# Retention attention and two MLPs in one kernel: where a chunk's small products, mask, state and key fade stand in a step

## The chip, the cores and the metric

The kernel runs on one core of one Trainium2 chip. The time is device microseconds (us) of one launch, the median of several runs. The engines are named as the profile names them: PE (TensorE, matrix products), PEld (its weight loads), DVE (VectorE), ACT (ScalarE), POOL (GpSimd) and SP (SyncE, which issues the DMAs). Each engine works through its own list of instructions in the order in which the program holds them.

## What is computed

The input is 2 batches of 8 heads with 768 positions of 64 features. Attention runs over blocks of 64 positions with a state per head that decays, and its output goes through two MLPs, one after the other (512 to 2048 to 512, 1536 tokens):

```python
for b in range(nb):                       # 12 blocks of 64 in a sequence
    intra = einsum('bhic,bhjc->bhij', qb, kb) * Dmask
    intra = einsum('bhij,bhjd->bhid', intra, vb)
    inter = einsum('bhid,bhde->bhie', qb * lam_pow, kv_state)
    out[:, :, sl] = intra + inter
    kb_dec = kb * rev_pow                 # the keys fade
    kv_state = lam_block * kv_state + einsum('bhsd,bhse->bhde', kb_dec, vb)

h = x @ w_in;  y = where(h > 0, h, exp(min(h, 0)) - 1) @ w_out      # first MLP
h = y @ w_in;  out = (P(h) / (Q(h) + 1e-6)) @ w_out                 # second MLP
```

## The kernel before, in words

The 1536 tokens are three tiles of 512. The hidden width of an MLP is 16 slices of 128, and one **step** is one slice `f` of one tile `t` of one layer: twelve 128x512 products make the slice `h` (`mlp_h`, line 424), ACT and DVE turn it into `ghi` and `glo` (two halves of the number, for precision), and two steps later twelve products add it to the four accumulators `y` (`mlp_y`, line 506). All products are taken three times, high by high, high by low and low by high.

The attention of the first token tile is done before any step. The attention of the other 1024 tokens, 16 chunks of 64 positions numbered 8 to 23, is laid into the first MLP's steps of `t = 0` and `t = 1`: a **visit** in a step starts chunk `n` and finishes the chunk `d` that the visit before had started. The steps with a visit are written out by hand: 3, 5, 7, 9, 10, 12, 13, 14, 15 for `t = 0` and 2, 4, 6, 8, 10, 12, 14, 15 for `t = 1`. A visit consists of

- `sm_products`: on PE, 64x64 products: keys by queries of `n` (line 332), values by masked scores of `d` (337), faded keys by values of `d` (343), state by queries of `d` (348). They go to two accumulator tiles, `aa`.
- `sm_mask(n)`: on DVE, the scores times the mask (line 368); `sm_decay_q(n)`: on POOL.
- `sm_out(d)`: on ACT, the state is scaled (four instructions, line 378) and the output is copied to `xr` (380); on DVE the new part is added to the state (384), which needs the scaled state and the products of line 343.
- `sm_decay_k(n)`: on ACT, the keys of `n` fade in place (four instructions, line 357). The products of line 343 in the next visit read them.

In the steps of `t = 0` the weights of the first MLP are made as well. They come as 64 bit numbers and are narrowed on DVE (lines 71, 74, 77), then copied on ACT (120) and subtracted on DVE (121). With the activation's own work (ACT lines 437, 438, 441; DVE 439, 442) that is the most work that DVE has in any stage. From step 10 a step makes two half pieces of weights.

The order of all engines in these steps is the order in which the code is written (`manual_schedule`). `run(ops, n)` issues the next `n` operations of a list: `old` holds what is left of the last step's activation (`b` on DVE, `ghi` on ACT, `glo` on DVE), `new` that of this step (`relu`, `exp` on ACT first), `lows` what is left of the last step's weights, and `now` this step's weights. In the kernel before, a step issues `h`; `b` and `ghi` of the step before; the fade of the keys that the last visit began; the first operation of the step's weights and what is left of the last ones; `glo`; `relu` and `exp`; then the visit; then the rest of the weights; and at its end `y` of two steps ago.

The DMAs stand in SP's list in the order of the code as well; the change moves none of them.

Of the kernel before, what the change touches and what calls it, by code (L numbers as in the profile page):

```python
# [29 lines left out]
def fused_kernel(ctx, tc, lam, qkv, w1, w2, ab, out):  # L30
# [5 lines left out]
    NF = w1.shape[0]  # L36
# [254 lines left out]
    chunk = {}  # L291
# [27 lines left out]
    def sm_products(n, d):  # L319

        if not aa_tiles:
            aa_tiles.extend(pa.tile([P, T], F32, tag=f"pa{i}", name=f"aa{i}")
                            .rearrange("p (x m i) -> p x m i", x=2, m=NP) for i in range(2))
            for r in ROWS:
                nc.tensor.matmul(aa_tiles[1][r, 1], lhsT=pick[r], rhs=mask64[r, :, 1:CS + 1],
                                 start=True, stop=True, skip_group_check=True)
            nc.scalar.activation(out=qpow[:, :, 0:CS], in_=aa_tiles[1][:, 1], func=AF.Copy)
        pn, pd = chunk.get(n), chunk.get(d)
        for m in range(NP):
            if pn:  # L330
                for r in ROWS:
                    nc.tensor.matmul(aa_tiles[0][r, 0, m], lhsT=pn["k"][r, m],  # L332
                                     rhs=pn["q"][r, m], start=True, stop=True,
                                     skip_group_check=True)
            if pd:
                for i, r in enumerate(ROWS):
                    nc.tensor.matmul(aa_tiles[1][ROWS[1 - i], 0, m], lhsT=pd["kv"][r, m, 1],
                                     rhs=pd["s"][r, m], start=m == 0, stop=d % KB == 0,
                                     skip_group_check=True)
        for m in range(NP):  # L340
            if pd and d % KB < KB - 1:
                for r in ROWS:
                    nc.tensor.matmul(aa_tiles[0][r, 1, m], lhsT=pd["kv"][r, m, 0],  # L343
                                     rhs=pd["kv"][r, m, 1], start=True, stop=True,
                                     skip_group_check=True)
            if pd and d % KB:
                for i, r in enumerate(ROWS):
                    nc.tensor.matmul(aa_tiles[1][ROWS[1 - i], 0, m], lhsT=state[r, m, 0],
                                     rhs=pd["q"][r, m], start=False, stop=True,
                                     skip_group_check=True)  # L350

    def sm_decay_k(n):

        kv = chunk[n]["kv"]
        if n % KB < KB - 1:
            for m in range(NP):
                nc.scalar.activation(out=kv[:, m, 0], in_=kv[:, m, 0], func=AF.Copy,
                                     scale=mask64[:, m, CS - 1:CS])

    def sm_decay_q(n):  # L360
        q = chunk[n]["q"]
        if n % KB:
            nc.gpsimd.tensor_tensor(out=q, in0=q, in1=qpow[:, :, 0:CS], op=ALU.mult)

    def sm_mask(n):
        b = chunk[n]
        b["s"] = s = ap_.tile([P, NP, CS], F32, tag="s", name=f"s{n}")
        nc.vector.tensor_tensor(out=s, in0=aa_tiles[0][:, 0], in1=mask64[:, :, 0:CS], op=ALU.mult)

    def sm_out(d):  # L370

        t, js = d * CS // T, slice(d * CS % T, d * CS % T + CS)
        if t not in xraw:
            xraw[t] = xr.tile([P, NP, T], F32, tag="xr", name=f"xr{t}")
        first, last = d % KB == 0, d % KB == KB - 1
        if not (first or last):
            for m in range(NP):
                nc.scalar.activation(out=state[:, m, 0], in_=state[:, m, 0], func=AF.Copy,  # L378
                                     scale=qpow[:, m, CS - 1:CS])
        nc.scalar.activation(out=xraw[t][:, :, js], in_=aa_tiles[1][:, 0], func=AF.Copy)  # L380
        if first:
            nc.scalar.activation(out=state[:, :, 0], in_=aa_tiles[0][:, 1], func=AF.Copy)
        elif not last:
            nc.vector.tensor_tensor(out=state[:, :, 0], in0=aa_tiles[0][:, 1],
                                    in1=state[:, :, 0], op=ALU.add)
# [17 lines left out]
    def x_split(layer, t, m):  # L403
        with tc.high_priority(HP):
            if m % 2 == 0:
                x_tiles(layer, t, m // 2)
            hi, lo = xs[layer, t, m]
            src = xraw[t][:, m] if layer == 0 else xraw.pop((t, m))
            split(hi, lo, src, nc.vector)
# [107 lines left out]
    with ExitStack() as actx:  # L517
# [61 lines left out]
        with tc.manual_schedule():  # L579
# [28 lines left out]
            def run(ops, n):  # L608
                for _ in range(n):
                    if ops:  # L610
                        ops.pop(0)()
# [75 lines left out]
        def steps(layer, t):  # L687
            return [(layer, t, f) for f in range(NF)]
# [3 lines left out]
        def att_visit(due, more):  # L692

            n = todo.pop(0) if more and todo else None
            d = due.pop() if due else None
            sm_products(n, d)
            if n is not None:
                sm_mask(n)
                sm_decay_q(n)
                due.append(n)  # L700
            if d is not None:
                sm_out(d)
                del chunk[d]

        with tc.manual_schedule():
            due = []
            faded = []
            lows = w
            old = []
            parks = [(f, i) for f in range(NF) if f not in DIRECT for i in range(2)]  # L710

            park_at = {(1, f): 2 if f in (5, 7, 9, 11) else 1 for f in (0, *range(3, NF - 2))}

            visits = [(3, 5, 7, 9, 10, 12, 13, 14, 15), (2, 4, 6, 8, 10, 12, 14, 15)]
            assert sum(park_at.values()) == len(parks)
            for layer, t, f in steps(0, 0) + steps(0, 1):
                if f == 0 and t:
                    mlp_y(*queue.pop(0))
                    for m in range(NP):
                        x_split(0, t, m)  # L720
                new = mlp_h(layer, t, f, later=True)
                queue.append((layer, t, f))
                if t or f != 1:
                    run(old, 2)
                    for n in faded:
                        sm_decay_k(n)
                    faded = []
                    now = []
                    if t == 0 and 0 < f < FULL:
                        now = [make_pair_ops(f)]  # L730
                        run(now[0], 1)
                    run(lows, 2 if t or f else 0)
                    for _ in range(park_at.get((t, f), 0)):
                        park_w2(*parks.pop(0))
                    if t == 0 and f >= FULL:
                        now = [make_half_ops(*h) for h in ((f + AHEAD, 0), (f, 1)) if h[0] < NF]
                        run(now[0], 1)
                    run(old, 1)
                    run(new, 2)
                    if f == 0 and t == 0:  # L740
                        run(lows, 1)
                        now = [lows]
                else:
                    now = [make_pair_ops(f)]
                    run(old, 1)
                    run(now[0], 1)
                    run(lows, 1)
                    run(old, 1)
                    run(lows, 2)
                    run(old, 1)  # L750
                    run(new, 2)
                    att_hand(*atts[-1])
                if f in visits[t]:
                    att_visit(due, t == 0 or f < NF - 1)
                    faded = list(due)
                for w in now if t or f else ():
                    run(w, len(w) - 1)
                if t == 0 and f + 2 < FULL:
                    load_pair(f + 2)
                elif t == 0 and f >= FULL:  # L760
                    load_raw(2 if f + 2 < NF else 1)
                if loads and (f in visits[t][1 - t:] or t == 0 and f < 2):
                    for load, k in loads.pop(0):
                        load(k)
                lows = [op for w in now for op in w]
                if len(queue) > LAG:
                    mlp_y(*queue.pop(0))
                old = new
            mlp_y(*queue.pop(0))
            for m in range(NP):  # L770
                x_split(0, 2, m)
            run(old, 3)
# [97 lines left out]
```

## Time and profile before

| | |
|---|---|
| median of 3 runs | 580.77 us (580.2 to 581.96) |
| profiled execution | 580.3 us, its span 578.5 us |
| busy over the span | PE 568.9 us (98%), DVE 468.6 us (81%), ACT 358.6 us (62%), POOL 25.2 us (4%) |
| steps of `t = 0` | from about 23 to 126 us of the span |
| steps of `t = 1` | from about 126 to 220 us |

The profile records one execution. A row of a timeline has the start and length of a group of instructions in us, the line of the code, what is written and read, the shape and the count; in square brackets stands how long the engine was idle before it and what it waited for.

### The profile page before, as it was taken

How to read it: one execution, taken by the hardware profiler on the slowest of the kernel's cores; microseconds unless marked ns; L12 is line 12 of the kernel's file. 1: busy time of each engine (PE TensorE's matmuls, PEld its weight loads, DVE VectorE, ACT ScalarE, POOL GpSimd, SP SyncE). 2: the span in 40 equal slices, each digit the busy share in tenths (PEclk: the TensorE clock that was granted, in tenths of full speed). 3: DMA queues.
4: the chain of work that ended last, by engine and by line, in shares of the span. 5: the costliest groups of instructions: out<-in, count | busy, mean ns of one | idle time of the engine just before them, and what ended most of it. 6: DMA issues, size and time to landing. Idle time of an engine off the chain costs nothing.

```text
span 578.5 us, 9311 instructions
## 1 busy us (share of the span) xinstructions
PE 568.9 (98%) x3570; PEld 468.0 (81%) x3570; DVE 468.6 (81%) x742; ACT 358.6 (62%) x687; POOL 25.2 (4%) x43
## 2 busy tenths in 40 slices
PE   8999999799999999999999999999999999999997
PEld 7878887688888888888888888888888888888885
DVE  6999999875667736677988899988898888898882
ACT  3555655666545535555568887676886676776662
POOL 5301000100001000000000000000000000000000
PEclk9999999899999999999999999999999999999999
DMA  8994546665677702553532410000310000200001
GB/s 304 317 271 166 189 122 201 185 178 164 181 251 229 213 25 74 195 187 128 180 110 92 164 36 2 0 1 1 114 32 2 0 1 0 75 1 1 0 1 73
DMA packets 41215, 64.58 MB, mean 112 GB/s; under 512 B 20178, under 2 KB 20178, under 8 KB 41170
## 3 DMA queue, kind: packets, MB, share of 16 engines
q1 hardware_dynamic: 41170, 63.98, 34.6%
q8 instruction: 28, 0.46, 0.3%
q14 instruction: 17, 0.14, 0.1%
HBM read 53.48 MB, written 10.49 MB: 111 GB/s over the span
## 4 chain that ended last, share of the span: by engine, by line
PE 83%; DVE 10%; DMA 2%; ACT 2%; issue 1%; SPq 1%; DVEq 0%; ACTq 0%
PE h L424 39%; PE y L506 37%; PE y L415 3%; DVE w L74 2%; DMA raw<-w_in 2%; DVE w L77 2%; DVE w L121 1%; DVE w L71 1%; ACT w L120 1%; PE aa L332 1%; DVE glo L442 1%; PE aa L343 1%; ACT state L378 1%; DVE b L439 0%; PE pa L195 0%
## 5 line engine op out<-in xcount | busy, mean ns | idle before, releaser
L424 PE MATMUL h<-xhi,w 128*128 128x512 f32 x768 | 205.1, 390 | 0.4 <-DVE w L121 0.4
L506 PE MATMUL y<-ghi,w 128*128 128x512 f32 x712 | 192.7, 393 | 0.0
L424 PEld LDWEIGHTS h<-xhi,w 128*128 128x128 f32 x768 | 143.8, 188 | 31.2 <-DVE w L121 0.9
L506 PEld LDWEIGHTS y<-ghi,w 128*128 128x128 f32 x712 | 132.8, 188 | 27.9
L424 PE MATMUL h<-xlo,w 128*128 128x512 f32 x384 | 102.7, 389 | 0.0
L506 PE MATMUL y<-glo,w 128*128 128x512 f32 x356 | 95.9, 391 | 0.0
L424 PEld LDWEIGHTS h<-xlo,w 128*128 128x128 f32 x384 | 72.1, 188 | 15.0
L506 PEld LDWEIGHTS y<-glo,w 128*128 128x128 f32 x356 | 67.4, 189 | 14.4
L450 ACT ACTIVATE a<-h,babs 128x512 f32<-128x512 f32 x48 | 33.0, 687 | 61.7 <-PE h L424 61.7
L437 ACT ACTIVATE a<-h 128x512 f32<-128x512 f32 x48 | 28.3, 589 | 43.8 <-PE h L424 43.7
L454 DVE SCALAR_TENSOR_TENSOR b<-b,babs,a 128x512 f32<-128x512 f32 x48 | 36.0, 750 | 19.9 <-ACT b L451 19.8
L439 DVE SCALAR_TENSOR_TENSOR b<-a,h 128x512 f32<-128x512 f32 x48 | 32.7, 681 | 13.8 <-ACT a L438 10.7
L441 ACT ACTIVATE ghi<-b 128x512 fp32r<-128x512 f32 x48 | 30.0, 627 | 22.2 <-DVE b L439 22.2
L120 ACT ACTIVATE w<-w 128x512 fp32r<-128x512 f32 (+1 forms) x23 | 18.4, 799 | 38.4 <-DVE w L77 38.4
L442 DVE TENSOR_TENSOR glo<-b,ghi 128x512 fp32r<-128x512 f32 x48 | 33.9, 709 | 7.0 <-ACT ghi L441 5.5
L452 ACT ACTIVATE p<-h,cab 128x512 f32<-128x512 f32 x48 | 37.7, 785 | 0.0
L456 ACT ACTIVATE a<-b,one 128x512 f32<-128x512 f32 x48 | 35.0, 729 | 3.4 <-DVE b L454 2.9
L458 DVE SCALAR_TENSOR_TENSOR p<-p,cab,h 128x512 f32<-128x512 f32 x48 | 35.8, 746 | 1.2
L462 DVE SCALAR_TENSOR_TENSOR b<-b,one,a 128x512 f32<-128x512 f32 x48 | 35.8, 746 | 0.1
L464 DVE SCALAR_TENSOR_TENSOR p<-p,cab,a 128x512 f32<-128x512 f32 x48 | 35.8, 746 | 0.0
L58 DVE TENSOR_TENSOR glo<-p,ghi 128x512 fp32r<-128x512 f32 x48 | 33.0, 688 | 3.0 <-PE y L415 1.5
L457 DVE TENSOR_TENSOR p<-p,h 128x512 f32<-128x512 f32 x48 | 32.8, 682 | 2.9 <-ACT p L452 2.9
(87 smaller groups left out, 631.0 us busy)
## 6 DMA issues: line engine op xcount, KB each, us to landing
raw<-w_in SPq DMA_DIRECT2D x64, 512.0 KB, 4.3
att<-qkv_in SPq DMA_DIRECT2D x16, 256.0 KB, 5.5
qk<-qkv_in SPq DMA_DIRECT2D x16, 256.0 KB, 3.9
kv<-qkv_in SPq DMA_DIRECT2D x64, 64.0 KB, 3.5
w2d<-wp SPq DMA_DIRECT2D x16, 256.0 KB, 4.3
w<-w2d SPq DMA_DIRECT2D x16, 256.0 KB, 2.7
x2d<-o SPq DMA_DIRECT2D x12, 256.0 KB, 2.2
x2r<-x2d SPq DMA_DIRECT2D x12, 256.0 KB, 3.3
```

Of the source, the lines that this page charges most:

```text
L58: lo_eng.tensor_tensor(out=lo, in0=src, in1=hi.bitcast(F32), op=ALU.subtract)
L424: nc.tensor.matmul(h, lhsT=w[:, a, 0, k * P:(k + 1) * P], rhs=xs[layer, t, k][b], start=i == k == 0, stop=i == 2 and k == NP - 1)
L442: lambda: nc.vector.tensor_tensor(out=glo, in0=b, in1=ghi.bitcast(F32), op=ALU.subtract)]
L450: nc.scalar.activation(out=a, in_=h, func=AF.Abs, scale=babs[:, 0:1])
L452: nc.scalar.activation(out=p, in_=h, func=AF.Identity, scale=cab[:, 3:4], bias=cab[:, 2:3])
L454: nc.vector.scalar_tensor_tensor(out=b, in0=b, scalar=babs[:, 1:2], in1=a, op0=ALU.mult, op1=ALU.add)
L456: nc.scalar.activation(out=a, in_=b, func=AF.Ln, bias=one[:, 0:1])
L457: nc.vector.tensor_tensor(out=p, in0=p, in1=h, op=ALU.mult)
L458: nc.vector.scalar_tensor_tensor(out=p, in0=p, scalar=cab[:, 1:2], in1=h, op0=ALU.add, op1=ALU.mult)
L462: nc.vector.scalar_tensor_tensor(out=b, in0=b, scalar=one[:, 0:1], in1=a, op0=ALU.add, op1=ALU.mult)
L464: nc.vector.scalar_tensor_tensor(out=p, in0=p, scalar=cab[:, 0:1], in1=a, op0=ALU.add, op1=ALU.mult)
L506: nc.tensor.matmul(ys[layer, t][m], lhsT=w[:, a, 1, m * P:(m + 1) * P], rhs=g[b], start=f == i == 0, stop=False)
```

## The change

Three things move, and no instruction is added or taken away. The visit's products stand ahead of the step's `h` on PE. The mask, the fade of the queries, the state and the copy to `xr` come as a list, `rest`, and are issued right after `b` and `ghi` of the step before, ahead of the step's weights and of `relu`. The fade of the keys, which stood in the step after the visit behind `ghi`, is issued at the end of the visit's own step, behind its weights (for the last visit of `t = 0`, at the end of the first step of `t = 1`).

```diff
             d = due.pop() if due else None
             sm_products(n, d)
+            rest = []
             if n is not None:
-                sm_mask(n)
-                sm_decay_q(n)
+                rest += [lambda: sm_mask(n), lambda: sm_decay_q(n)]
                 due.append(n)
             if d is not None:
-                sm_out(d)
-                del chunk[d]
+                rest += [lambda: sm_out(d), lambda: chunk.pop(d)]
+            return rest
...
+                rest = att_visit(due, t == 0 or f < NF - 1) if f in visits[t] else []
                 new = mlp_h(layer, t, f, later=True)
                 queue.append((layer, t, f))
                 if t or f != 1:
                     run(old, 2)
-                    for n in faded:
-                        sm_decay_k(n)
-                    faded = []
+                    while rest:
+                        rest.pop(0)()
                     now = []
...
-                if f in visits[t]:
-                    att_visit(due, t == 0 or f < NF - 1)
-                    faded = list(due)
                 for w in now if t or f else ():
                     run(w, len(w) - 1)
+                if f in visits[t] and f < NF - 1 or f == 0 and t:
+                    for n in due:
+                        sm_decay_k(n)
```

Two places show what that does to the engines' lists. The first is DVE and ACT around step 5 of `t = 0`, which has a visit. `b_0_4`, `ghi_0_4` and `glo_0_4` belong to the activation of step 4, `w_4` and `w_5` are weights, `s` is the masked score, `a_0_5` the activation of step 5 (lines 437 and 438 are `relu` and `exp`). DVE before:

```order
L439 SCALAR_TENSOR_TENSOR b_0_4_674<-a_0_4_673,h_0_4_658 128x512
L71 TENSOR_SCALAR w_5_726<-raw_5_643 128x1024
L121 TENSOR_TENSOR w_4_681<-w_4_682,w_4_681 128x1024
L442 TENSOR_TENSOR glo_0_4_672<-b_0_4_674,ghi_0_4_671 128x512
L368 TENSOR_TENSOR s_764<-aa_624,dmask 128x256
L384 TENSOR_TENSOR state<-aa_624,state 128x4x64
L74 SCALAR_TENSOR_TENSOR w_5_726<-raw_5_643,w_5_726 128x1024
```

DVE now:

```order
L439 SCALAR_TENSOR_TENSOR b_0_4_678<-a_0_4_677,h_0_4_662 128x512
L368 TENSOR_TENSOR s_757<-aa_598,dmask 128x256
L384 TENSOR_TENSOR state<-aa_598,state 128x4x64
L71 TENSOR_SCALAR w_5_768<-raw_5_647 128x1024
L121 TENSOR_TENSOR w_4_681<-w_4_682,w_4_681 128x1024
L442 TENSOR_TENSOR glo_0_4_676<-b_0_4_678,ghi_0_4_675 128x512
L74 SCALAR_TENSOR_TENSOR w_5_768<-raw_5_647,w_5_768 128x1024
```

The mask and the add to the state stand directly behind `b`; three operations that stood ahead of them now stand behind. ACT at the same place, before:

```order
L120 ACTIVATE w_4_681<-w_4_682 128x1024
L441 ACTIVATE ghi_0_4_671<-b_0_4_674 128x512
L437 ACTIVATE a_0_5_721<-h_0_5_706 128x512
L438 ACTIVATE a_0_5_721<-a_0_5_721 128x512
L378 ACTIVATE state<-state,qpow 128x64 x4
L380 ACTIVATE xr_767<-aa_625 128x4x64
```

and now:

```order
L120 ACTIVATE w_4_681<-w_4_682 128x1024
L441 ACTIVATE ghi_0_4_675<-b_0_4_678 128x512
L378 ACTIVATE state<-state,qpow 128x64 x4
L380 ACTIVATE xr_760<-aa_599 128x4x64
L437 ACTIVATE a_0_5_753<-h_0_5_738 128x512
L438 ACTIVATE a_0_5_753<-a_0_5_753 128x512
```

The scaling of the state still stands behind `ghi` of step 4, which reads what `b` wrote. The second place is steps 12 and 13 of `t = 0`, which both have a visit: visit 12 begins chunk 13, and visit 13 reads its keys. ACT before, where `kv_1135` holds the keys of chunk 13:

```order
L120 ACTIVATE w_12_1231<-w_12_1_1233 128x512
L441 ACTIVATE ghi_0_12_1223<-b_0_12_1226 128x512
L357 ACTIVATE kv_1135<-kv_1135,dmask 128x64 x4
L437 ACTIVATE a_0_13_1310<-h_0_13_1295 128x512
L438 ACTIVATE a_0_13_1310<-a_0_13_1310 128x512
L378 ACTIVATE state<-state,qpow 128x64 x4
```

and now, where they are `kv_1139`:

```order
L120 ACTIVATE w_12_1260<-w_12_1_1262 128x512
L357 ACTIVATE kv_1139<-kv_1139,dmask 128x64 x4
L441 ACTIVATE ghi_0_12_1247<-b_0_12_1250 128x512
L378 ACTIVATE state<-state,qpow 128x64 x4
L380 ACTIVATE xr_760<-aa_599 128x4x64
L437 ACTIVATE a_0_13_1346<-h_0_13_1331 128x512
```

The fade has passed one instruction, `ghi`; it still stands behind the copy of the last weights of step 12. PE at the same place, from the end of step 12 on, before:

```order
L506 MATMUL y_0_3_585<-ghi_0_10_1083,w_10_1090 128x512
L424 MATMUL h_0_13_1295<-xhi_0_0_263,w_11_1180 128x512 x2
L424 MATMUL h_0_13_1295<-xhi_0_1_299,w_11_1180 128x512 x2
...
L332 MATMUL aa_624<-qk_1140 64x64 x2
L337 MATMUL aa_625<-s_1262,kv_1135 64x64 x2
...
L343 MATMUL aa_624<-kv_1135 64x64 x2
L348 MATMUL aa_625<-qk_923,state 64x64 x2
```

and now:

```order
L506 MATMUL y_0_3_585<-ghi_0_10_1107,w_10_1117 128x512
L332 MATMUL aa_598<-qk_1144 64x64 x2
L337 MATMUL aa_599<-s_1253,kv_1139 64x64 x2
...
L343 MATMUL aa_598<-kv_1139 64x64 x2
L348 MATMUL aa_599<-qk_927,state 64x64 x2
...
L424 MATMUL h_0_13_1331<-xhi_0_0_263,w_11_1180 128x512 x2
L424 MATMUL h_0_13_1331<-xhi_0_1_299,w_11_1180 128x512 x2
```

The twelve products of `h` that stood between the end of step 12 and the read of the faded keys now stand behind that read.

## Rows read from the trace of the kernel before

**Rows 1.** Waits of PE: engine, line, releaser; us in total, times, longest

```profile
PE aa L343 <- ACT kv L357: 3.4, 1, 3.4
```

**Rows 2.** Windows: length, busy us and instructions by engine, clock, DMA share, GB/s

```profile
27.00:80.00 53.00, 52.55 (x425) 41.84 (x425) 50.25 (x62) 31.58 (x67) 3.28 (x4) 1.00 0.72 212
80.00:99.00 19.00, 19.00 (x170) 15.45 (x169) 17.03 (x27) 10.16 (x20) 0.73 (x1) 1.00 0.51 155
...
105.00:109.00 4.00, 4.00 (x32) 3.16 (x29) 2.78 (x6) 2.60 (x9) 0.00 (x0) 0.57 0.50 140
...
110.00:225.00 115.00, 115.00 (x1059) 93.75 (x1058) 73.41 (x128) 61.72 (x152) 7.34 (x9) 1.00 0.59 177
```

**Rows 3.** Chain of waits from 20 to 110 us, its shares by line

```profile
by line: DMA raw<-w_in 15.3%; DVE w L74 14.9%; DVE w L77 12.8%; DVE w L121 7.8%; issue 6.9%; ACT w L120 5.4%; DVE w L71 5.1%; PE y L506 4.9%; DVE glo L442 4.9%; ACT state L378 3.4%; DVE b L439 3.2%; SPq L315 2.6%; ACT ghi L441 1.7%; ACT a L
```

**Rows 4.** Timeline of PE, end of step 12 to step 14

```profile
94.84 1.19 PE L506 MATMUL y<-ghi,w 128*128 128x512 f32 x4
...
97.70 1.07 PE L424 MATMUL h<-xhi,w 128*128 128x512 f32 x4
...
100.51 0.27 PE L332 MATMUL aa<-qk 64*64 64x64 f32 x2
...
104.60 0.27 PE L343 MATMUL aa<-kv 64*64 64x64 f32 x2 [3.40 <-ACT kv L357]
...
105.72 2.07 PE L506 MATMUL y<-ghi,w 128*128 128x512 f32 x4
...
110.01 1.08 PE L424 MATMUL h<-xhi,w 128*128 128x512 f32 x4
...
113.35 0.23 PE L343 MATMUL aa<-kv 64*64 64x64 f32 x2
```

**Rows 5.** Timeline of DVE, steps 4 to 13

```profile
48.55 0.68 DVE L442 TENSOR_TENSOR glo<-b,ghi 128x512 fp32r<-128x512 f32 x1
...
51.54 0.68 DVE L439 SCALAR_TENSOR_TENSOR b<-a,h 128x512 f32<-128x512 f32 x1
...
54.50 0.42 DVE L368 TENSOR_TENSOR s<-aa,dmask 128x256 f32<-128x256 f32 x1
55.37 0.42 DVE L384 TENSOR_TENSOR state<-aa,state 128x256 f32<-128x256 f32 x1 [0.46 <-ACT state L378]
...
67.30 0.42 DVE L384 TENSOR_TENSOR state<-aa,state 128x256 f32<-128x256 f32 x1 [0.46 <-ACT state L378]
...
79.22 0.42 DVE L384 TENSOR_TENSOR state<-aa,state 128x256 f32<-128x256 f32 x1 [0.28 <-ACT state L378]
...
83.16 1.23 DVE L121 TENSOR_TENSOR w<-w,w 128x1024 fp32r<-128x1024 f32 x1 [0.53 <-ACT w L120]
...
107.40 0.42 DVE L384 TENSOR_TENSOR state<-aa,state 128x256 f32<-128x256 f32 x1 [1.17 <-ACT state L378]
```

**Rows 6.** Timeline of ACT, steps 4 to 14

```profile
47.28 0.61 ACT L441 ACTIVATE ghi<-b 128x512 fp32r<-128x512 f32 x1
47.79 1.05 ACT L357 ACTIVATE kv<-kv,dmask 128x64 f32<-128x64 f32 x4
48.75 0.58 ACT L437 ACTIVATE a<-h 128x512 f32<-128x512 f32 x1
...
52.63 0.61 ACT L441 ACTIVATE ghi<-b 128x512 fp32r<-128x512 f32 x1
53.15 0.58 ACT L437 ACTIVATE a<-h 128x512 f32<-128x512 f32 x1
...
54.29 1.05 ACT L378 ACTIVATE state<-state,qpow 128x64 f32<-128x64 f32 x4
...
103.68 0.63 ACT L441 ACTIVATE ghi<-b 128x512 fp32r<-128x512 f32 x1
104.22 1.05 ACT L357 ACTIVATE kv<-kv,dmask 128x64 f32<-128x64 f32 x4
...
112.11 1.05 ACT L357 ACTIVATE kv<-kv,dmask 128x64 f32<-128x64 f32 x4
```

More of the change, by code (lines that the diff above doesn't have):

```diff
@@ L724, in fused_kernel @@
                     run(old, 2)
-                    for n in faded:
-                        sm_decay_k(n)
-                    faded = []
+                    while rest:
+                        rest.pop(0)()
                     now = []
```

## The prediction, made before the changed kernel was run

> **What bounds the kernel now.** I read the waits of PE first. After the start-up PE stops once for more than half a us, for 3.4 us, before the products of line 343, and what it waits for there is the fade of the keys on ACT, line 357 [rows 1]. From that point on it runs without a break, and the end of the kernel is this run's end. So whatever makes PE late up to that point is paid in full, and nothing else is.
>
> The second view is the windows. DVE works 50.25 of 53.00 us from 27 to 80 us and 17.03 of 19.00 us from 80 to 99 us, but only 73.41 of 115 us from 110 to 225 us [rows 2]. PE looks as full as DVE in the first two, but it is not what sets the pace: the chain of waits from 20 to 110 us is made of DVE's weight lines 74, 77, 121 and 71, of the weights' DMAs and of ACT's lines 120 and 378, with PE's `y` at 4.9% [rows 3]. PE started the stage with work in hand, and DVE falls behind it step by step until at step 13 PE has used up its lead. I read the timelines around that point last.
>
> There, PE finishes `y` (94.84 to 97.70) and `h` (97.70 to 100.51, 2.81 us), issues the first part of visit 13 and waits from about 101.2 until the first of the four fades of chunk 13 is done: 104.60 [rows 4]. On ACT that fade stands behind `ghi` of step 12, which starts at 103.68; the fade itself starts at 104.22 [rows 6]. [...]
>
> **The change, part by part.** The work of PE is the same, and each `h` and `y` has a visit before it as often as before, so the order on PE costs nothing where PE doesn't wait. SP's list keeps its order. In `t = 1` DVE has a third of its time free [rows 2], and its visits are two steps apart but for the last; I take nothing there. What is left is `t = 0`.
>
> *The add to the state.* On DVE it now stands right behind `b` and the mask, ahead of weights that need nothing from it. It needs the scaled state, and the scale on ACT stands behind `ghi`, which in turn needs `b`. In step 5: `b` starts at 51.54 and takes 0.68, the mask 0.42 [rows 5], so DVE is at the add at 52.64. On ACT `ghi` starts at 52.63, and the next instruction at 53.15 [rows 6]; the scale now comes there, takes 1.05 [rows 6], and the add can start at about 54.22. DVE idles 1.58 us. Before, the add stood behind three more operations and idled 0.46 [rows 5]: 1.12 us more. Step 7 has the same spacing and the same 0.46, step 9 the same spacing with 0.28, so 1.30 [rows 5]. Together 3.5 us. The visit of step 10 has no add, since it finishes a sequence; there the mask fills 0.3 us of a wait of 0.53 us [rows 5]. Net 3.2 us. From below, a visit costs nothing more if the scale could be ready when DVE arrives; nothing in the lists allows that, since the scale can't pass `ghi`. From above, the rows' lengths overlap a little at their ends, so that DVE may be there some 0.1 us earlier in each visit.
>
> [...] The row shows that DVE stood still for 0.46 us before the add although weight operations were behind it [rows 5]. [...]
>
> *The fade ahead of `ghi`.* The four fades take 0.96 us until the next instruction (47.79 to 48.75) and now stand ahead of `ghi`. In step 4 `ghi` moves from 47.28 to 48.24 and ends at 48.85 with its 0.61 [rows 6]; `glo` on DVE, which reads it, started at 48.55 [rows 5] and now waits 0.3 us. That happens in steps 4, 6 and 8: 1.0 us. From below it is nothing, if DVE arrives later for another reason.
>
> So DVE, and with it ACT, is 4.2 us later at step 12 than before.
>
> *Visit 13.* The fade gains the place of `ghi`, 104.22 to 103.68, 0.54 us [rows 6]. But the products stand ahead of `h` now. PE arrives at the fade 0.7 us (100.51 to 101.2) after 97.70, at about 98.4 instead of 101.2 [rows 4], and can't do `h` while it waits; `h`, 2.81 us, which before ran ahead of the wait, comes after it. So the end of the step moves by 4.2 - 0.54 + 2.81 = 6.5 us. Bounds of this term by itself: 2.27 us if DVE is not late at all.
>
> *Visits 14 and 15.* Both follow a step with a visit. DVE's mask now waits for PE. In step 13, `b` is done when `ghi` starts, 103.68 [rows 6]; the products end 1.12 us after 104.06 (104.60 to 105.72 [rows 4]), at 105.18; the mask ends at 105.6, the scale 1.05 later than 105.18, and the add starts at about 106.25. DVE idles 1.5 + 0.65 = 2.2 us where it idled 1.17 [rows 5]: another 1.0 us. The fade for visit 14 began at 112.11 [rows 6] and is now at 112.11 + 4.2 - 0.54 + 1.0 = 116.8, its four parts done from 117.1 to 117.9. PE comes to it at 113.35 [rows 4] + 6.5 - 2.81 = 117.0, and the four pairs of products wait for the four parts, 0.4 to 0.5 us in all. Visit 15 repeats this. Together 0.9 us; nothing from below, if the lists leave the 0.6 us that they lack, and 2 us from above, DVE's whole loss in two steps.
>
> [...]
>
> **Sum.** 4.2 + 2.3 + 0.9 = 7.4 us on the profiled 580.3: 587.7. The median of the runs is 0.5 above the profiled execution, so 588.2.
>
> **Rivals.**
> - *DVE's loss is swallowed.* DVE waits for DMAs in this stage too (15.3% of the chain [rows 3]); if these waits shrink by as much as the others grow, only 2.3 remain: 583.1. Against it: a DMA of raw weights goes out when DVE frees its buffer, so it moves with DVE. Chance 0.12.
> - *A second cold stretch.* [...] Chance 0.14. [...]
> - *Faster: the stall goes.* The fade is issued a step earlier in the code. [...] The point that decides is the copy of the last weights of step 12 on ACT: the fade stands right behind it and can't start before 103.68, and PE comes at 98.4. DVE would have to be 5.3 us earlier. Chance 0.06.
> - *No difference.* The change is made of moves on engines with slack but for DVE: 580.8. It needs gains and losses to cancel. Chance 0.04.
>
> **The numbers.** The main case has 0.64, with 585.5 to 590 as its own range. The range of 583.5 to 592 takes in the cold stretch, 2 us for visits 14 and 15, and most of the case in which part of DVE's loss is swallowed; outside it are a little under 0.2. A difference of 0.3%, 1.7 us, is about what a measurement of this kernel can tell from none. Faster 0.06, same 0.04, slower 0.90.
>
> **What would show it.** In the profile after: a wait of PE before line 343 at visit 13 of 5 us or more, now ahead of `h`; waits of DVE before line 384 in steps 5, 7 and 9 of about 1.6 us, released by line 378; short waits of `glo` for `ghi` in steps 4, 6, 8; DVE 4 us later at step 12; 0.3 to 0.5 us waits of PE before line 343 in steps 14 and 15; no new wait from 130 us on. It is wrong if DVE at step 12 is as early as before, or if PE at visit 13 finds the keys faded.

## The result, and the profile after

The changed kernel takes 589.63 us (588.37 to 590.62, 4 runs) against 581.37 us (580.2 to 582.16, 4 runs) of the kernel before on the same chip: a ratio of 1.0139 [1.0118, 1.0159], 1.4% slower. The forecast was 588.2 us. The profiled execution took 588.37 us with a span of 586.6 us, where the one of before took 580.3 and 578.5: 8.1 us more in the span, and these 8.1 us are what has to be found.

The waits of PE, in the view that [rows 1] are taken from (line, releaser, us in total, times, longest):

```profile
PE aa L343 <- ACT kv L357: 5.8, 1, 5.8
PE h L424 <- DVE w L121: 1.5, 2, 0.8
...
PE aa L332 <- DVE state L384: 0.8, 1, 0.8
PE aa L332 <- ACT state L382: 0.5, 1, 0.5
```

The one wait for the faded keys has grown from 3.4 to 5.8 us. The other three lines are small: two are new, and line 424 waited 0.4 us before. All of them lie ahead of that wait, so they take from it and not from the end: a PE that comes earlier to line 343 waits there longer, until the same fade is done.

The windows (length, busy us and instructions of PE, PEld, DVE, ACT, POOL, then clock, DMA share, GB/s), against [rows 2]:

```profile
27.00:80.00 53.00, 51.49 (x416) 40.83 (x415) 47.89 (x58) 28.64 (x60) 5.50 (x4) 1.00 0.66 205
...
105.00:109.00 4.00, 0.31 (x12) 0.31 (x15) 3.23 (x6) 1.86 (x5) 0.00 (x0) 0.50 0.43 154
109.00:115.00 6.00, 6.00 (x44) 4.80 (x37) 4.53 (x9) 2.09 (x8) 0.00 (x0) 0.51 0.40 117
130.00:225.00 95.00, 95.00 (x854) 77.52 (x853) 57.30 (x100) 49.19 (x120) 5.13 (x7) 1.00 0.60 176
```

DVE, which sets the pace from 27 to 80 us, does 2.36 us less work in these 53 us (47.89 against 50.25, 58 instructions against 62). From 105 to 109 us PE works 0.31 of 4.00 us at half the clock (0.50), and from 109 to 115 us it is busy throughout, still at half (0.51). The forecast and the expectations call such a stretch cold; in the kernel before, with 0.57 from 105 to 109 us [rows 2], the `y` that began in it took 4.29 us, 1.43 more than the 2.86 of the `y` of the step before [rows 4]. From 130 us on it is busy 95.00 of 95.00 us: nothing is lost there.

The timeline of DVE shows where its work went; the brackets give the idle time ahead of an instruction and its releaser:

```profile
48.89 0.89 DVE L442 TENSOR_TENSOR glo<-b,ghi 128x512 fp32r<-128x512 f32 x1 [0.25 <-ACT ghi L441]
52.69 0.42 DVE L368 TENSOR_TENSOR s<-aa,dmask 128x256 f32<-128x256 f32 x1
54.77 0.42 DVE L384 TENSOR_TENSOR state<-aa,state 128x256 f32<-128x256 f32 x1 [1.67 <-ACT state L378]
...
68.42 0.42 DVE L384 TENSOR_TENSOR state<-aa,state 128x256 f32<-128x256 f32 x1 [1.67 <-ACT state L378]
...
82.06 0.42 DVE L384 TENSOR_TENSOR state<-aa,state 128x256 f32<-128x256 f32 x1 [1.67 <-ACT state L378]
...
103.09 0.93 DVE L71 TENSOR_SCALAR w<-raw 128x512 int32<-128x512 int32 x1 [0.63 <-DMA raw<-w_in]
```

Steps 5, 7 and 9 lose 1.67 us each before the add, where they lost 0.46, 0.46 and 0.28 [rows 5]; `glo` waits 0.25 us in step 4. The last row is a wait for a DMA, 0.63 us in step 12. All of DVE's waits from 27 to 105 us (us in total, times, longest):

```profile
DVE state L384 <- ACT state L378: 5.0, 3, 1.7
DVE w L71 <- DMA raw<-w_in: 1.5, 3, 0.7
DVE glo L442 <- ACT ghi L441: 0.7, 3, 0.3
DVE w L121 <- ACT w L120: 0.2, 1, 0.2
```

The same view of the kernel before has 1.2 us for the add (three times), 0.5 for line 121, none for `glo`, and for the DMA

```profile
DVE w L71 <- DMA raw<-w_in: 2.5, 3, 1.3
```

so that DVE waits 7.4 us in this stretch where it waited 4.2. Of the 1.0 us by which the waits for the DMA are shorter, 0.55 lie at one wait at about 35 us and are made up again by step 4, whose `b` starts at 46.19 before and at 46.20 now; from there on DVE waits 1.2 us for the DMA before and 0.8 now. The timeline of ACT says why the add waits, and when the keys of chunk 13 are ready:

```profile
53.17 0.61 ACT L441 ACTIVATE ghi<-b 128x512 fp32r<-128x512 f32 x1
53.69 1.05 ACT L378 ACTIVATE state<-state,qpow 128x64 f32<-128x64 f32 x4
...
107.77 0.63 ACT L120 ACTIVATE w<-w 128x512 fp32r<-128x512 f32 x1 [1.16 <-DVE w L77]
108.30 1.05 ACT L357 ACTIVATE kv<-kv,dmask 128x64 f32<-128x64 f32 x4
```

The scale starts 0.52 us after `ghi` and the add 1.08 us after the scale, while DVE was done with the mask at about 53.1. The fade stands right behind the copy of the last weights and begins at 108.30; it was at 104.22 [rows 6]. Last PE, from the end of step 12 on, against [rows 4]:

```profile
102.19 0.27 PE L332 MATMUL aa<-qk 64*64 64x64 f32 x2 [0.54 <-ACT state L382]
...
108.69 0.37 PE L343 MATMUL aa<-kv 64*64 64x64 f32 x2 [5.81 <-ACT kv L357]
...
109.83 2.07 PE L424 MATMUL h<-xhi,w 128*128 128x512 f32 x4
...
115.02 1.09 PE L506 MATMUL y<-ghi,w 128*128 128x512 f32 x4
...
117.87 0.27 PE L332 MATMUL aa<-qk 64*64 64x64 f32 x2
...
134.32 1.07 PE L424 MATMUL h<-xhi,w 128*128 128x512 f32 x4
```

Line 343 starts at 108.69 where it started at 104.60: 4.1 us. Step 13 ends at 117.87, 9.18 us later; before it ended at 110.01, 5.41 us later: 3.8 us. The last row shown is the first `h` of `t = 1`. In the kernel before it was

```profile
126.27 1.07 PE L424 MATMUL h<-xhi,w 128*128 128x512 f32 x4
```

so it is now 8.05 us later, and the steps 14 and 15 added only 0.2 us. 4.1 + 3.8 + 0.2 = 8.1, the whole difference of the spans.

### The profile page after: what moved, and what is told of

Same layout as the page of the kernel before. It is cut to its first block, busy times and chain, and to the rows that moved or that the text cites. A ratio compares the mean times of both kernels' runs of the same rounds, so it can differ in the third digit from the quotient of the medians.

```text
span 586.6 us, 9301 instructions
## 1 busy us (share of the span) xinstructions
PE 572.7 (98%) x3570; PEld 471.3 (80%) x3570; DVE 468.0 (80%) x742; ACT 358.5 (61%) x687; POOL 26.3 (4%) x43
## 4 chain that ended last, share of the span: by engine, by line
PE 82%; DVE 8%; DMA 4%; ACT 2%; issue 1%; SPq 1%; ACTq 0%; DVEq 0%
PE h L424 39%; PE y L506 36%; PE y L415 3%; DMA raw<-w_in 2%; DVE w L74 2%; DVE w L77 2%; DVE w L121 1%; DVE glo L442 1%; DMA att<-qkv_in 1%; DVE w L71 1%; PE aa L332 1%; PE aa L343 1%; ACT w L120 1%; DMA kv<-qkv_in 1%; SPq L178 1%
## 5 line engine op out<-in xcount | busy, mean ns | idle before, releaser
L424 PE MATMUL h<-xhi,w 128*128 128x512 f32 x768 | 208.7, 395 | 1.5 <-DVE w L121 1.5
L506 PE MATMUL y<-ghi,w 128*128 128x512 f32 x712 | 189.7, 389 | 0.0
```

What stands on the lines that cost most here:

```text
L424: nc.tensor.matmul(h, lhsT=w[:, a, 0, k * P:(k + 1) * P], rhs=xs[layer, t, k][b], start=i == k == 0, stop=i == 2 and k == NP - 1)
L506: nc.tensor.matmul(ys[layer, t][m], lhsT=w[:, a, 1, m * P:(m + 1) * P], rhs=g[b], start=f == i == 0, stop=False)
```

## Experiments

They came in three batches, each on a chip of its own and beside its own runs of the kernel before: 581.87 us for e1 to e4, 581.7 for e5 to e8, 581.51 for e9 to e12. The ratios given are to these. The theory was that of the forecast: DVE loses by the add's new place, PE loses because `h` no longer covers the wait for the keys. The rivals were that the fade's place alone does it, that the clock does it, and that DMAs stand behind all of it.

### The parts of the change: e1, e2, e3

e1 does one part alone, on the kernel before:

```diff
-                    for n in faded:
-                        sm_decay_k(n)
-                    faded = []
...
                     att_visit(due, t == 0 or f < NF - 1)
-                    faded = list(due)
                 for w in now if t or f else ():
                     run(w, len(w) - 1)
+                if f in visits[t] and f < NF - 1 or f == 0 and t:
+                    for n in due:
+                        sm_decay_k(n)
```

> Of the three moves only the fade of the keys is made: it is issued at the end of the visit's step, ahead of ghi; products, mask and state stay where they were before. Theory of the prediction: the fade gains the 0.54 us of ghi at visit 13, and glo waits 0.25 us in steps 4, 6 and 8 (0.8 us in all), so 0.2 to 0.5 us slower than before, about 581.7; the wait of PE before line 343 stays at 3.4 to 3.9 us and stands behind h. Rival 1: an earlier fade takes the wait away, 576.5. Rival 2: most of the 8.3 us of the change come from the fade standing ahead of ghi, 586 or more.

Measured 583.13 us, 1.0025 [1.0008, 1.0043]. The wait before line 343 stays at 3.3 us; there is a second of 1.5 us before line 332. The fade's new place by itself brings nothing and costs about 1.3 us, where 0.2 to 0.5 were expected. That is little more than the measurement can tell from none, and in the profiled execution DVE waited 2.5 us for raw weights from 40 to 105 us, where the kernel before waited 1.2.

e2 keeps the products ahead of `h`, but puts mask, state and copy back behind `relu` and `exp`:

```diff
                     run(old, 2)
-                    while rest:
-                        rest.pop(0)()
                     now = []
...
                     att_hand(*atts[-1])
+                while rest:
+                    rest.pop(0)()
                 for w in now if t or f else ():
```

> The changed kernel with mask, queries' fade, state and x back behind relu and exp of the step; the products ahead of h and the fade at the end of the step stay. Theory of the prediction, term by term: DVE's adds wait as little as before, so its 3.2 us go, and 1.0 for glo, 2.3 for h behind the wait, 0.9 for visits 14 and 15 and the longer cold stretch stay: about 586. Rival: the moves hang together. With the products at the head of a step, the mask and the state of the visit before must be through by then, and where visits stand in consecutive steps (9 and 10, 12 to 15) the products wait for DVE: waits of 2 us each before lines 332 and 343 at visits 10, 14 and 15, and a time as long as that of the changed kernel or longer, 589.5 to 592.

Measured 597.84 us, 1.0279 [1.0257, 1.03]: both the theory and the rival missed, by 5.8 us and more. The timeline of ACT in step 13, and of DVE there and in the two steps behind it:

```profile
113.97 0.60 ACT L437 ACTIVATE a<-h 128x512 f32<-128x512 f32 x1 [4.37 <-PE h L424]
...
115.14 1.05 ACT L378 ACTIVATE state<-state,qpow 128x64 f32<-128x64 f32 x4
```

```profile
116.22 0.42 DVE L384 TENSOR_TENSOR state<-aa,state 128x256 f32<-128x256 f32 x1 [5.57 <-ACT state L378]
...
129.44 0.42 DVE L384 TENSOR_TENSOR state<-aa,state 128x256 f32<-128x256 f32 x1 [5.94 <-ACT state L378]
...
139.99 0.42 DVE L384 TENSOR_TENSOR state<-aa,state 128x256 f32<-128x256 f32 x1 [5.61 <-ACT state L378]
```

`relu` needs the step's `h`, `h` now stands behind the visit's products, and these wait for the fade. So the scale behind `relu` comes very late, DVE stands still for 5.6 to 5.9 us in three steps, and PE's waits before line 343 are 8.5 us in three. The change's two moves belong together: with the products ahead, "rest ahead" is worth 8.2 us (597.84 against 589.63), although it is what makes DVE wait 1.67 us in steps 5, 7 and 9.

e3 shortens that wait alone: in the changed kernel the scale goes to the head of the step, ahead of `ghi`.

```diff
+                done = due[:1] if f in visits[t] else []
...
                 if t or f != 1:
+                    for d in done:
+                        sm_scale(d)
                     run(old, 2)
```

> The changed kernel with the four scalings of the state (line 378 there, in its own function here) issued on ACT at the head of the step, ahead of ghi, so that DVE's add finds them done. Theory of the prediction: the waits of DVE before the add in steps 5, 7 and 9 fall from 1.67 us to under 0.5, DVE is 3 to 3.5 us earlier at step 12, and all of that is won at visit 13: 586 to 587. Rival (the DMAs of the weights set DVE's pace, its waits are swallowed): the waits fall, the time stays at 589 to 590.

Measured 587.55 us, 1.0097 [1.0077, 1.0116], 2.1 us below the changed kernel's median. In the timeline of DVE, steps 5 and 12:

```profile
54.45 0.42 DVE L384 TENSOR_TENSOR state<-aa,state 128x256 f32<-128x256 f32 x1 [1.15 <-ACT state L372]
...
103.09 0.47 DVE L71 TENSOR_SCALAR w<-raw 128x512 int32<-128x512 int32 x1 [1.89 <-DMA raw<-w_in]
```

The add still waits 1.15 us, not the expected 0.5 or less, since the scale now stands behind the copy of the last weights (line 120). The waits of the three steps are 3 x 0.52 = 1.6 us shorter, and the median is 2.1 us lower: it lies between the theory (586 to 587) and the rival (589 to 590), so DVE's wait before the add is paid at the end in the main. In the profiled execution most of it was lost again. Line 71 of step 12 starts at 103.09 in both kernels, here after 1.89 us of waiting for the raw weights, there after 0.63. On SP the group of loads that begins with the one for that line starts, in the changed kernel and in e3,

```profile
98.52 9.57 SPq L107 DMA_DIRECT2D raw<-w_in  x4
```

```profile
97.26 10.37 SPq L107 DMA_DIRECT2D raw<-w_in  x4
```

so the load was sent 1.26 us earlier, and line 71 started 5.8 us behind it instead of 4.6. The load went out earlier with DVE, but how long DVE waits there changes from one execution to the next (0.63 to 2.21 us with the same program up to it: e4 and e12, below).

### Where in the run: e7 and e8

The new order in steps up to 12 of `t = 0` only (e7), and from step 13 on only (e8):

```diff
+                ahead = t == 0 and f < 13
+                rest = att_visit(due, t == 0 or f < NF - 1) if f in visits[t] and ahead else []
...
-                if f in visits[t]:
-                    att_visit(due, t == 0 or f < NF - 1)
-                    faded = list(due)
+                if f in visits[t] and not ahead:
+                    for op in att_visit(due, t == 0 or f < NF - 1):
+                        op()
```

The cut is against the kernel before. In e8 the first line reads `ahead = t or f >= 13`; the fade is at the end of the step in both.

> Half of the change: in steps 3 to 12 of t = 0 as in the changed kernel, in visits 13 to 15 of t = 0 and in t = 1 products behind h, and mask, state and x behind relu and exp, as before; the fade at the end of the step everywhere. Theory of the prediction: DVE's 4.2 us less the 0.54 of ghi stay, h runs ahead of the wait again, so its 2.81, the 0.9 of visits 14 and 15 and the longer cold stretch go: before + 3.7, 585.3. Rival (the loss is made at the consecutive visits alone): within 1.5 us of before, 581.5 to 583.

> The other half: steps 3 to 12 of t = 0 with products behind h and the rest behind relu and exp, as before; visits 13 to 15 of t = 0 and all of t = 1 as in the changed kernel; the fade at the end of the step everywhere. Theory of the prediction: h behind the wait 2.81, less 0.54 for ghi, 0.8 for glo, 0.9 for visits 14 and 15, 0.9 for the longer cold stretch: before + 4.9, 586.5. Rival (the loss is DVE's adds in steps 5 to 9, the place of h is nothing): 581.5 to 583.

Measured 585.82 us, 1.0085 [1.0065, 1.0105], and 586.17 us, 1.0084 [1.0066, 1.0101]. Both expectations held. The halves cost 4.1 and 4.5 us, together 8.6 against 8.3 for the whole. The fade's move is in both; counted once, with the 1.3 us of e1, they make 7.3. By the intervals of the three runs, about 1 us each, both sums fit the whole. The waits of PE in e7, the longest line:

```profile
PE aa L343 <- ACT kv L357: 4.2, 1, 4.2
```

and in e8:

```profile
PE aa L332 <- ACT state L382: 4.1, 1, 4.1
PE aa L343 <- ACT kv L357: 3.3, 1, 3.3
```

In e7 `h` still runs ahead of the wait, and PE waits because DVE, and with it the fade, is late. In e8 nothing ahead of step 13 has a new place but the fade, and PE loses by its own order: it stands at the visit's products twice, with `h` behind both waits. The first of these waits comes from the seam between the two orders (in the changed kernel it is 0.5 us), but the second ends with the fade in any case.

### The clock: e4 and e12

Both fill PE's wait at visit 13 of the changed kernel with products of 128x256 whose result nobody uses, 28 in e4 and 44 in e12:

```diff
+        for _ in range(44 if d == 13 else 0):
+            nc.tensor.matmul(aa_tiles[1][:, 1].rearrange("p m i -> p (m i)"), lhsT=wt[0, 11][:, 0, 0, 0:P], rhs=xs[0, 0, 0][0][:, 0:NP * CS],
+                             start=False, stop=True, skip_group_check=True)
```

The lines below them are shifted by three: 343 is 346 here, 357 is 360, 424 is 427.

> The changed kernel with 28 extra 128x256 products on PE at visit 13, between the products of lines 337 and 343, where PE waits 5.8 us; they go to a part of an accumulator that is not read again, so they add work whose result is not used. [...]

> The changed kernel with 44 instead of 28 extra 128x256 products in PE's wait at visit 13, so that some 5.2 of the 5.8 us are filled; their result is not used. With 28 they took 3.6 us, 2.3 us of idle time were left, and a cold stretch of 3.4 us came all the same, later and in the products of h and y. Theory: idle time under 1 us brings no lower clock, h of step 13 takes 2.8 us instead of 5.2, and the time falls by 1.5 to 2.5 us to 587 to 588. Rival: DVE sets the pace through steps 13 to 15 and hides what the clock costs: 589 to 590.5.

e4: 589.76 us, 1.0139 [1.0111, 1.0167]. The products ended while PE still had 2.3 us to wait, and the clock fell all the same, later (0.74 from 109 to 115 us). That says nothing on what the clock costs. e12: 590.75 us, 1.015 [1.0116, 1.0185]. Its windows and the two groups that count on PE's timeline:

```profile
103.00:109.00 6.00, 5.66 (x58) 5.39 (x48) 4.98 (x8) 1.53 (x4) 0.74 (x1) 1.00 0.29 96
109.00:115.00 6.00, 5.98 (x54) 4.97 (x55) 4.19 (x8) 3.67 (x11) 0.00 (x0) 1.00 0.52 136
```

```profile
110.02 1.19 PE L427 MATMUL h<-xhi,w 128*128 128x512 f32 x4
...
112.87 1.07 PE L509 MATMUL y<-ghi,w 128*128 128x512 f32 x4
...
117.83 0.27 PE L346 MATMUL aa<-kv 64*64 64x64 f32 x2 [1.46 <-ACT kv L360]
...
118.82 0.96 PE L427 MATMUL h<-xhi,w 128*128 128x512 f32 x3
```

At the full clock (1.00) `h` of step 13 takes 2.85 us (110.02 to 112.87) and not 5.19. But PE then waits 1.46 us for the fade of the next chunk, and `h` of step 14 starts at 118.82, in the changed kernel at 118.97. In the profiled executions the gain is 0.2 us (588.18 against 588.37), not 1.5 to 2.5: DVE and ACT set the pace through steps 13 to 15, and the PE at half clock mostly spent what it would have waited. Line 71 of step 12 started 0.5 us later in this execution than in that of the changed kernel (103.59 against 103.09), so that much of a gain may be hidden in it. The median, 1.1 us above the changed kernel's and 0.25 above the rival's range, says less than it seems to: in two of e12's four executions (591.73 and 591.96 us) the mean clock was 0.996, so, by that mean, some stretch at a lower clock was in them too. The other two, at 1.000, took 588.18 and 589.78 us, within the 588.37 to 590.62 of the changed kernel, whose clock was 0.991 to 0.994. A gain of 2 us is not there; one below 1 us can't be ruled out.

The changed kernel, e4 and e12 have the same program up to that line, and yet DVE waited there for the raw weights 0.63, 1.62 and 2.21 us. A difference of a us in this one wait is no effect of an edit.

### The fade early, and what stands behind it: e5, e6, e9, e10, e11

Line 343 waits since the fade stands on ACT behind the copy of weights that DVE makes. e5 puts it inside the visit, right behind the state and the copy, in the order of before; e6 does the same to the changed kernel (behind `relu` and `exp`):

```diff
                     att_visit(due, t == 0 or f < NF - 1)
-                    faded = list(due)
+                    for n in due:
+                        sm_decay_k(n)
                 for w in now if t or f else ():
```

> The kernel before with one move: the fade of the keys is issued inside the visit, right behind state and x and so ahead of the step's copies of weights on ACT, which wait for DVE. Theory: at visit 12 ACT has some 2 us of slack there and the keys have landed, so they are faded when PE comes to visit 13; its wait of 3.4 us and the cold stretch of 1.43 us behind it go, DVE's lateness shows in small waits elsewhere: 577 to 578.5 against 581.6 before. Rival: at visits 13 and 14 the keys of the new chunk have only just been sent for, ACT waits for their DMA with the copies of the weights behind it, and the gain goes there: 580.5 to 582.

> The changed kernel with the fade issued right behind relu and exp of the visit's step, ahead of the copies of the weights. Theory of the prediction: PE's wait at visit 13 falls from 5.8 us to about 1 and the cold stretch behind it (2.3 us) goes; DVE's losses at the adds stay and show as waits of PE for keys, masks or weights: 583.5 to 585.5. Rival: DVE's lateness is what PE waits for in any case, so that the wait only moves to other lines: 587 to 589.5.

e5: 581.95 us, 0.9996 [0.9977, 1.0015], the rival's number. e6: 590.42 us, 1.0155 [1.0131, 1.018]: the theory missed by 5 us, the rival by 1. The waits of PE in e5, its longest line, and the two fades on ACT's timeline:

```profile
PE aa L332 <- DMA qk<-qkv_in: 3.2, 2, 2.5
```

```profile
110.04 1.07 ACT L357 ACTIVATE kv<-kv,dmask 128x64 f32<-128x64 f32 x4 [1.09 <-DMA kv<-qkv_in]
...
117.51 1.06 ACT L357 ACTIVATE kv<-kv,dmask 128x64 f32<-128x64 f32 x4 [1.17 <-DMA kv<-qkv_in]
```

The wait before line 343 is gone from e5, the clock is 1.00 from 103 to 115 us, and the time has not moved: PE waits 3.2 us for the DMA of the next chunk's queries and keys, and ACT for that of the keys and values. The same lines of e6:

```profile
PE aa L332 <- DMA qk<-qkv_in: 5.2, 2, 4.6
PE h L424 <- DVE w L121: 2.6, 3, 1.2
PE aa L337 <- DMA kv<-qkv_in: 2.0, 1, 2.0
```

The chunk's loads stand in SP's list behind the loads of raw weights, which wait for a buffer that DVE must free (from 84 to 112 us of the kernel before, SP waits there 14.1 us for line 71). e10 turns the two around on the kernel before, and nothing else; e9 is e5 with that, e11 is e6 with it:

```diff
-                elif t == 0 and f >= FULL:
-                    load_raw(2 if f + 2 < NF else 1)
                 if loads and (f in visits[t][1 - t:] or t == 0 and f < 2):
...
                         load(k)
+                if t == 0 and f >= FULL:
+                    load_raw(2 if f + 2 < NF else 1)
```

> The control to the run above: the kernel before with the order of these loads alone. Theory: PE's wait at visit 13 is for the fade behind the copies of the weights, not for loads; it stays at 3.4 us, 581 to 582.5. Rival: the loads alone give the gain, 577 to 579; or raw weights are late, 583 and more.

> The kernel with the fade inside the visit, products and state in the order of the kernel before, and in steps 10 to 15 the loads of the next chunk's keys, values and queries ahead of the loads of raw weights on SP, which wait there for DVE. Theory: the wait of 3.4 us for the fade at visit 13 only moved to waits for the next chunk's DMAs, on PE 2.5 us for queries at visit 15 and on ACT 1.1 and 1.2 us for keys, because these loads stand behind raw loads that wait for DVE; with them ahead, nothing takes the place of the wait: 576.5 to 578.5. Rival: raw weights come later by the 2.5 to 3.8 us that SP needs for the six loads, DVE waits that much more for them in steps 11 and 12, and the time stays at 581 to 583.

> The changed kernel with both, the fade right behind relu and exp and the loads first. Theory: of the 8.3 us of the change, what hangs on the fade at visit 13 goes (PE's wait of 5.8 us with h behind it, the long cold stretch), and no DMA takes its place as it did with the fade alone; DVE's waits at the adds in steps 5, 7 and 9 stay and show at weights, masks and state, 2.5 to 4 us: 582.5 to 585. Rival: DVE's lateness is in the end of the stage anyway: 588 to 590.

The times of all three lie in the theory's ranges. e10: 581.16 us, 1.0005 [0.9983, 1.0026] (PE's wait before line 343 was 2.2 us at visit 13 in its profile, not 3.4, and 0.8 us at visit 15), so the order of the loads alone is worth nothing. e9: 578.06 us, 0.9928 [0.9904, 0.9952], 3.5 us faster than before and the fastest of all. e11: 584.87 us, 1.0055 [1.0035, 1.0075], 4.8 us below the changed kernel. The waits of PE in e9 and its window from 105 to 109 us:

```profile
PE aa L332 <- DVE state L384: 1.0, 1, 1.0
PE h L424 <- DVE w L121: 1.0, 1, 1.0
```

```profile
105.00:109.00 4.00, 4.00 (x78) 3.16 (x76) 3.63 (x9) 3.48 (x12) 0.39 (x1) 1.00 0.67 193
```

PE is busy 4.00 of 4.00 us, where it worked 0.31 in the changed kernel, and at a clock of 1.00, where the kernel before had 0.57 and the changed kernel 0.50. The waits of PE in e11:

```profile
PE h L424 <- DVE w L121: 3.0, 3, 1.2
PE aa L332 <- DVE state L384: 1.8, 2, 1.2
...
PE aa L343 <- ACT kv L357: 1.1, 2, 0.7
```

With the same two cures the new order is still 6.8 us behind e9, and its longest waits are now for DVE. The cures together take 3.5 us off the kernel before and 4.8 us off the changed kernel; neither gains by the fade alone (e5, e6). So the late fade explains little of the difference between the two orders by itself: of the 8.3 us of the change 6.8 are left when the keys come in time. The forecast's terms that need no late fade, 4.2 us for DVE and 0.9 for visits 14 and 15, make 5.1 of them; the other 1.7 us are not explained by these runs.

## Why the prediction was right or wrong, point by point

- **What bounds the kernel, and that only lateness at visit 13 counts:** right for these two kernels. The span grew by 8.1 us, the first `h` of `t = 1` came 8.05 us later, and PE ran without a break behind it. e9 shows the other side: with that wait gone, and the loads behind it, the kernel is 0.7% faster than before.
- **The add to the state, 3.5 us:** 1.67 us against 0.46, 0.46 and 0.28 make 3.8. The spacing from `ghi` over the scale to the add was read rightly, and step 10's mask fills a wait as forecast (0.53 to 0.20). Two weight operations (lines 71 and 121), which ran without a wait when they stood there before, stood behind the add, and DVE started neither while it stood still for 1.67 us: in step 5 its rows come in the order of its list (`b` 52.09, mask 52.69, add 54.77, line 71 55.11, line 121 55.71).
- **The fade ahead of `ghi`, 1.0 us:** 0.25, 0.24 and 0.24, so 0.7.
- **DVE and ACT 4.2 us later at step 12, the fade 0.54 us earlier in its list:** the sum, 3.66, measured 4.08 (104.22 to 108.30): DVE's `b` of step 12 is 4.68 us later (102.97 to 107.65), and the fade gains 0.60. From `b` of step 4 on, the waits alone make 3.8: 3.8 for the add, 0.7 for `glo`, less 0.3 for line 121 and 0.4 for the DMA. The other 0.9 are lengths of single instructions, on which the forecast had nothing: the three `glo` that wait take 0.89 or 0.90 us instead of 0.68 (0.6 in all), line 71 of step 12 0.93 instead of 0.43, and others are shorter. That the waits and the lengths together come close to the forecast's 4.2 is in part luck. e7, which has this half and the fade's move, cost 4.1 us in the median.
- **`h` behind the wait, 2.81 us:** the step that the sum rests on, and right in kind: from line 343 to the end of step 13 it is 3.77 us more. The excess is the clock (0.50 to 0.51 up to 115 us). `h` took 5.19 us (109.83 to 115.02) instead of 2.81, and the `y` behind it 2.85 (115.02 to 117.87) instead of 4.29: 2.81 + 2.38 - 1.44 = 3.75.
- **Visits 14 and 15, 0.9 us:** 0.2, and PE does not wait there. The forecast 2.81 + 0.9 = 3.7 and the measured 3.77 + 0.2 = 4.0 stand for the same time: the half clock spent what PE would have waited at visit 14. e12 bears it out: at a clock of 1.00 the wait is there, 1.46 us, and `h` of step 14 starts within 0.2 us of the same time.
- **The clock, and a second cold stretch (0.14):** the sum has no term for the clock, which is wrong in the profile and nearly right in the time. The stretch was longer, 9.9 us at half clock from 105 to 115 us against 3.4 before, and `h` took 2.4 us more in it; but by e12's profile that cost 0.2 us at the end, or 0.7 with line 71's 0.5 us. The four executions of the changed kernel point the same way: the two with the lower mean clock, 0.991, took 588.37 and 589.39 us, the two with 0.994 589.87 and 590.62.
- **The swallowed loss (0.12):** 0.4 of the 4.2 us by which DVE's other waits grew, in the profiled execution (1.2 us of waits for the DMA from step 4 on before, 0.8 after); that is less than this wait changes between executions, so it is not shown to come from the change. There was never more than 1.2 to take in that stretch, which the share of 15.3% of the chain [rows 3] hid: it counts the transfers, not DVE's waits.
- **Faster, the stall goes (0.06):** the point named was that the fade stands behind the last weights' copy. It does, and e5 shows that even without it the time stays, because the DMAs of the next chunk come next (PE waits 3.2 us for its queries and keys). That second limit was not seen in the forecast or ahead of e6; only the rival of e5 named it.

So the mechanism was right and the sum 0.7 us short in the span: 0.4 at the fade's start, 0.3 in the steps behind it. What stays open is how the 6.8 us between e11 and e9 divide between the add and the other moves, and why DVE waits 0.63 us for the raw weights of step 12 in one execution and 2.21 in another.

## What to carry to other kernels

Work that an engine can do while something else is late is cover, and a waiting instruction that is moved ahead of it puts all of it on the path: `h` cost nothing ahead of the wait, and behind it its 2.8 us stood in the sum in full. On the engine that sets the pace, an instruction is worth no earlier place than its slowest input allows: the add held DVE up for 1.67 us in each of three steps. And when a wait is taken away and the time does not move, look for the next wait and cure both: in the order of before the fade alone gave 0.9996, the loads alone 1.0005, both 0.9928.

## What the runs showed of the hardware that was not expected

The granted clock fell around PE's long waits, and stayed low with PE busy again. After 3.4 us of idling it was 0.57 over 4 us [rows 2], so at half for about 3.4 of them; around the wait of 5.81 us, 0.50 and 0.51, so at half for about 9.9 of the 10 us from 105 to 115, the last 6 of them with PE busy; in windows of one us both kernels have 0.50 at the lowest. With the wait filled but for 2.3 us (e4) it still fell, to 0.74 from 109 to 115 us; with 5.53 us of products and 0.36 us of waiting left (e12) it did not in the profiled execution (1.00 from 103 to 115 us).

One wait for a DMA, DVE's for the raw weights at step 12, came out as 0.63, 1.62 and 2.21 us in three executions with the same program up to it (e4 and e12 on different chips), which is as much as some terms of the forecast.
